# TensorE's per-quad work as a loop of three turns, with the values of the last two quads in other PSUM banks, in a sliding-window attention decode step

## The chip, the cores and the metric

The kernel runs on one core of a Trainium2 chip. The metric is the device time of one execution in microseconds (us).

## The reference

One token for each of 32 sequences attends to the last 512 positions of a cache of 2,048. There are 32 query heads over 8 key/value heads of width 128; all arrays are bfloat16.

```python
W = min(4096, max(256, Sk // 4))                      # 512
q = (x @ wq).reshape(B, Sq, Hq, Dh)...                # x 32x1x512, wq 512x4096
k = jnp.repeat(k_cache[:, :, Sk - W:, :], rep, axis=1)   # 32 x 8 x 512 x 128, rep 4
v = jnp.repeat(v_cache[:, :, Sk - W:, :], rep, axis=1)
p = softmax(einsum("bhqd,bhkd->bhqk", q, k) * Dh ** -0.5)
out = einsum("bhqk,bhkd->bhqd", p, v)... @ wo         # wo 4096x512
```

## The kernel before

The 32 sequences are worked on in eight quads of four. A quad's window of keys is one load of 4 MB (K), its window of values another (V). In both, the 128 partitions are sequence, key/value head and a quarter of the window: each partition holds 128 rows of 128 elements. `K_sb` and `V_sb` have two buffers each, for even and odd quads. `V_sb[1]` first holds the query weights (two loads of 2 MB at the very start), and `K_sb[0]` holds the output weights (4 MB as W0, W1 and W2) at the end.

For each quad q the steps have letters, which the orders use:

- T (VectorE, line 445): 32x32 transposes of K into `KT_sb`, in two halves `Tq.0` and `Tq.1`, both of which read the whole buffer.
- GpSimd (line 289) lays the queries of the quad out as a block diagonal `QBD`, two buffers.
- S (TensorE, line 331): scores in two halves, 16 matmuls each, into one PSUM bank `S_ps`.
- M, X, N: maximum (VectorE, 451, 453), exponential with row sums (ScalarE, 496), normalised probabilities as bfloat16 (VectorE, 457, 459).
- E (TensorE, 346): 16 matmuls that bring the probabilities to the rows of the values, into `EP_ps`; G (ScalarE, 503) copies them out.
- B (VectorE 465, ScalarE 509): eight instructions spread them into the block-diagonal `bd`, two buffers.
- P (TensorE, 361): probabilities times values, 128 matmuls in 32 groups of four; `P4.8.24` is groups 8 to 23 of quad 4. They accumulate in four banks `O_ps`.
- C (VectorE 470, ScalarE 514): four copies pick each head's own part out into `C_sb`, two buffers.
- F (TensorE, 373) and D (ScalarE, 518): four float32 matmuls fold the picks into one bank `F_ps`, and a copy puts them into `o_sel` as columns for the output projection.

After all quads TensorE multiplies `o_sel` by the output weights (line 393: 64 matmuls for W0, 48 for W1, 16 for W2), VectorE and ScalarE copy the result out, and SP stores it.

The order on each engine is written out by hand in the strings `PE_OPS`, `DVE_OPS` and `ACT_OPS`; TensorE's, VectorE's and ScalarE's programs are those strings unrolled. `needs()` gives the steps that an operation has to wait for, `ends` the value that a step's counting semaphore has when it is done, and `Waits` emits a wait only where an engine has not yet waited for as much. Loads are issued by SP alone, in the order of `LOADS`, and SP waits in that order too: a K of quad 2 or later waits for the second transpose half two quads before (line 228), a V for the last P two quads before (236), V1 for the query projection, and W0 for `T6.1` (242).

```python
LOADS = """
K0 K1 V0.0 K2 V1.0 K3 V2.0 K4 V3.0 K5 K6 V4.0 K7 V5.0 V5.1 V6.0 V6.1 V7.0 V7.1 W0 W1 W2
""".split()
V_PIECES = [1, 1, 1, 1, 1, 2, 2, 2]
```

So V0 to V4 come in one piece, V5 to V7 in halves. The eight PSUM banks are: scores 0, E 1, values 2 to 5, folds 6, output projection 7.

Of the kernel before, what the change touches and what calls it, by code (L numbers as in the profile page):

```python
# [17 lines left out]

PE_OPS = """
S0.0 S0.1 S1.0 S1.1 E0 E1 P0.0.32 S2.0 F0 S2.1 P1.0.12 E2 P1.12.32 F1 S3.0 S3.1 P2.0.12 E3  # L20
P2.12.32 F2 S4.0 S4.1 P3.0.12 E4 P3.12.32 S5.0 S5.1 S6.0 P4.0.4 E5 P4.4.8 S6.1 P4.8.24 E6 P4.24.32
F3 S7.0 P5.0.20 S7.1 P5.20.32 E7 F4 P6.0.32 F5 P7.0.32 F6 F7
"""
DVE_OPS = """
T0.0 T0.1 T1.0 M0 T1.1 N0 M1 N1 B0.0.4 B1.0.4 T2.0 T2.1 M2 N2 B2.0.4 T3.0 T3.1 M3 N3 B3.0.4 T4.0
T4.1 M4 N4 B4.0.4 T5.0 C3.2.3 T5.1 C3.3.4 T6.0 M5 T6.1 N5 B5.0.4 M6 N6 T7.0 C4.2.4 T7.1 B6.0.4 M7
N7 C5.2.4 B7.0.5 C6.2.4 C7.2.4
"""
ACT_OPS = """
X0 X1 G0 B0.4.8 G1 B1.4.8 C0.0.4 D0 X2 G2 B2.4.8 C1.0.4 D1 X3 G3 B3.4.8 C2.0.4 D2 X4 G4 B4.4.8  # L30
C3.0.2 X5 G5 B5.4.8 X6 G6 C4.0.2 B6.4.7 D3 B6.7.8 X7 C5.0.2 G7 B7.5.6 D4 B7.6.8 C6.0.2 D5 C7.0.2
D6 D7
"""
# [14 lines left out]
def bass_standalone__sliding_block_cached__sampling_kernel(  # L48
# [8 lines left out]
    B, Sq, D = x.shape  # L57
# [14 lines left out]

    orders = {"PE": ops_of(PE_OPS), "DVE": ops_of(DVE_OPS), "ACT": ops_of(ACT_OPS)}

    ends, total = {}, {}
    for eng, ops in orders.items():
        for op in ops:
            kind = op[0]
            total[eng, kind] = total.get((eng, kind), 0) + 1
            if kind in "BC":  # L80
                for i in range(op[2], op[3]):
                    ends[kind, op[1], i] = (eng, kind, total[eng, kind])
            elif kind == "P":
                for g in range(op[2], op[3]):
                    ends["P", op[1], g] = (eng, kind, total[eng, kind])
            else:
                ends[op] = (eng, kind, total[eng, kind])

    def needs(op):
        kind, q = op[0], op[1]  # L90
        spread = lambda q: [("B", q, h) for h in range(HKV)]
        picks = lambda q: [("C", q, r) for r in range(4)]
        d = []
        if kind == "T":
            d = [("S", q - 1, op[2])]
        elif kind == "S":
            d = [("T", q, op[2]), ("X", q - 1)]
        elif kind == "M":
            d = [("S", q, 1)]
        elif kind == "X":  # L100
            d = [("M", q), ("N", q - 1)]
        elif kind == "N":
            d = [("X", q), ("E", q - 1)]
        elif kind == "E":
            d = [("N", q), ("G", q - 1)]
        elif kind == "G":
            d = [("E", q)] + spread(q - NG)
        elif kind == "B":
            d = [("G", q), ("P", q - 2, 31)]
        elif kind == "P":  # L110
            d = spread(q) + picks(q - 1)
        elif kind == "C":
            d = [("P", q, 31), ("F", q - 2)]
        elif kind == "F":
            d = picks(q) + [("D", q - 1)]
        elif kind == "D":
            d = [("F", q)]
        return [ends[n] for n in d if n[1] >= 0]

    with ExitStack() as es:  # L120
# [47 lines left out]
        sem_v = [[sem(f"sem_v{i}_{j}") for j in range(max(V_PIECES))] for i in range(2)]  # L168
        sem_wo = [sem(f"sem_wo{i}") for i in range(len(WOP))]
        sem_out = sem("sem_out")  # L170
        names = (
            "pe_xT pe_q pe_Y dve_xT dve_q dve_QT dve_m dve_r dve_y dve_c act_q act_y act_warm "
            "pool_x pool_e pool_ei pool_q pool_f pool_m pool_j pool_qbd pool_fz"
        ).split()
        s = {n: sem(n) for n in names}
        op_sem = {key: sem("op_%s_%s" % key) for key in total}

        def v_waits(q, g0, g1):

            n = V_PIECES[q]  # L180
            for i in range(n):
                if g0 <= i * 32 // n < g1:
                    c = sum(1 for p in range(q % 2, q + 1, 2) if V_PIECES[p] > i)
                    yield i * 32 // n, sem_v[q % 2][i], 16 * c

# [33 lines left out]
        def _(sp):  # L219
# [3 lines left out]
            for op in ops_of(" ".join(LOADS)):  # L223
# [5 lines left out]
                elif kind == "V":  # L229
                    if q == 1:  # L230
                        sp.wait_ge(s["pe_q"], 8)
                    if q >= 2:
                        wait([ends["P", q - 2, 31]])
                    n = R // V_PIECES[q]
                    r0 = op[2] * n
                    sp.dma_start(  # L236
                        V_sb[q % 2][:, r0 * DH:(r0 + n) * DH], rows(v_cache, q, r0, r0 + n)
                    ).then_inc(sem_v[q % 2][op[2]], 16)
                else:
                    wait([ends["T", NQ - 2, 1]])  # L240
                    i0, i1 = WOP[q]
                    sp.dma_start(  # L242
                        wo_sb[:, i0:i1, :].rearrange("p i n -> p (i n)"),
                        wo_r[:, i0:i1, :].rearrange("p i n -> p (i n)"),
                    ).then_inc(sem_wo[q], 16)
# [8 lines left out]
        def _(pool):  # L254
# [27 lines left out]
            for q in range(NQ):  # L282
                if q >= 2:
                    wait([ends["S", q - 2, 1]])
                for b in range(4):
                    pr = slice(32 * b, 32 * b + 32)
                    if q or b:
                        pool.wait_ge(s["pool_qbd"], 4 * q + b)
                    pool.tensor_copy(  # L289
                        QBD[pr, q % 2].rearrange("p (w t) (h c) -> p w t h c", w=2, h=HKV)[  # L290
                            :, :, :, :, 4 * b:4 * b + 4],
                        QT_sb[pr, q].rearrange("p w (h e) t -> p w t h e", h=HKV),
                    ).then_inc(s["pool_qbd"], 1)

        @block.tensor
        def _(pe):
# [23 lines left out]
            def scores(q, w):  # L320
                if w == 0:
                    pe.wait_ge(s["pool_qbd"], 4 * q + 4)
                if q == 0 and w == 0:
                    pe.wait_ge(s["dve_q"], 4)
                    pe.wait_ge(s["act_q"], 4)
                for t in range(2):
# [232 lines left out]
```

## Time and profile before

| | |
|---|---|
| Timed runs (3) | 186.43 us median, 186.42 to 186.54 |
| Profiled execution: span from first to last instruction | 184.68 us (184.7 on the page) |
| Profiled execution's own total | not listed apart; the median of the timed runs is 1.75 us over the span |
| Busy: TensorE, its weight loads | 119.1 us (65%), 56.8 us (31%) |
| Busy: VectorE, ScalarE, GpSimd | 106.6 us (58%), 49.8 us (27%), 16.9 us (9%) |
| Mean granted TensorE clock | 0.823 |
| Moved by DMA | 75.80 MB in 3,584 packets, mean 410 GB/s |
| Costliest groups | transposes T 70.6 us (16 of 4.43 us), P 63.1 us (1,024 matmuls), S 25.3 us (256) |

Busy time is the time in which an engine has an instruction at work. The chain is the work that ended last, followed back from step to step to what released it. Queue q1 holds the kernel's loads and its store, q10 the loads of x, and the two queues of kind "instruction" bring program code to the engines. PE is TensorE, PEld its weight loads, DVE VectorE, ACT ScalarE, POOL GpSimd, SP SyncE.

### The profile page before, as it was taken

The numbers are of one execution on the slowest core, as the hardware profiler recorded it, in microseconds if no ns is written. First come the engines' busy times: TensorE is split into PE (matmuls) and PEld (weight loads), VectorE is DVE, ScalarE is ACT, GpSimd is POOL, SyncE is SP. The second block draws the span as 40 slices with busy tenths as digits, with TensorE's granted clock in tenths as the row PEclk, the third lists the DMA queues.
The fourth block names the chain that finished last, engine by engine and source line by source line (L and its number), as shares of the span: only waits on it lengthen the run. The fifth ranks groups of instructions, "written<-read, shape, count | busy, mean of one in ns | idle before, by whom it ended". The sixth has DMA issues, their size and how long they took to land.

```text
span 184.7 us, 3662 instructions
## 1 busy us (share of the span) xinstructions
PE 119.1 (65%) x1636; PEld 56.8 (31%) x1636; DVE 106.6 (58%) x106; ACT 49.8 (27%) x93; POOL 16.9 (9%) x52
## 2 busy tenths in 40 slices
PE   0089104447696795549944992441799899888872
PEld 0034000014452351304431350000345445444362
DVE  0031999994549631973299327999646996302031
ACT  3001300011935157001650162001062704502031
POOL 7900040202000200002000200020000000000000
PEclk9999955555599999657987699555579999999999
DMA  6999999999999999999999999999999999999970
GB/s 217 415 490 390 426 454 454 433 390 426 451 447 429 405 422 447 440 436 397 421 451 447 433 397 426 447 440 426 419 429 405 426 426 422 440 412 429 423 299 30
DMA packets 3584, 75.80 MB, mean 410 GB/s; under 512 B 432, under 2 KB 496, under 8 KB 624
## 3 DMA queue, kind: packets, MB, share of 16 engines
q1 hardware_dynamic: 3504, 75.53, 95.9%
q8 instruction: 13, 0.21, 0.5%
q10 hardware_dynamic: 64, 0.03, 0.1%
q14 instruction: 3, 0.02, 0.0%
HBM read 75.53 MB, written 0.03 MB: 409 GB/s over the span
## 4 chain that ended last, share of the span: by engine, by line
DMA 77%; DVE 13%; issue 3%; PE 3%; SPq 3%; DVEq 0%
DMA K_sb<-in_k_cache_dram 49%; DMA V_sb<-in_v_cache_dram 15%; DMA K_sb<-in_wo_dram 13%; DVE KT_sb L445 12%; PE ps L361 2%; SPq L236 1%; SPq L228 1%; SPq L242 1%; PE ps L331 1%; SPq L193 0%; DVE C_sb L470 0%; DVE maxv L451 0%; PE ps L393 0%; DVEq L120 0%; DVE P_bf L479 0%
## 5 line engine op out<-in xcount | busy, mean ns | idle before, releaser
L445 DVE STREAM_TRANSPOSE KT_sb<-K_sb 128x4096 f32<-128x4096 f32 x16 | 70.6, 4433 | 12.5 <-DMA K_sb<-in_k_cache_dram 12.4
L361 PE MATMUL ps<-V_sb,bd 32*128 32x512 bf16 x1024 | 63.1, 397 | 4.7 <-DMA V_sb<-in_v_cache_dram 2.9
L331 PE MATMUL ps<-KT_sb,QBD 128*32 128x512 bf16 x256 | 25.3, 532 | 39.7 <-DVE KT_sb L445 30.0
L361 PEld LDWEIGHTS ps<-V_sb,bd 32*128 32x128 bf16 x1024 | 27.0, 97 | 38.1 <-issue 12.3
L331 PEld LDWEIGHTS ps<-KT_sb,QBD 128*32 128x32 bf16 x256 | 6.6, 114 | 56.1 <-DVE KT_sb L445 37.0
L496 ACT ACTIVATE P_f<-ps,negmax 128x512 f32<-128x512 f32 x8 | 5.5, 687 | 63.1 <-DVE negmax L453 63.1
L509 ACT ACTIVATE bd<-PTc,mask 128x512 bf16<-128x512 bf16 x31 | 20.1, 710 | 0.3
L514 ACT ACTIVATE C_sb<-ps 32x512 f32<-32x512 f32 x22 | 12.9, 587 | 25.6 <-PE ps L361 25.4
L289 POOL COPY QBD<-QT_sb 32x128 bf16<-32x128 bf16 x32 | 9.2, 287 | 106.6 <-PE ps L331 90.2
L465 DVE TENSOR_SCALAR bd<-PTc,mask 128x512 bf16<-128x512 bf16 x33 | 9.3, 348 | 13.8 <-ACT PTc L503 13.8
L470 DVE COPY C_sb<-ps 32x512 f32<-32x512 f32 x10 | 6.9, 693 | 15.7 <-PE ps L361 15.6
L373 PE MATMUL ps<-C_sb,F_sb 128*128 128x128 f32 x64 | 10.0, 303 | 6.3 <-ACT C_sb L514 5.7
L346 PE MATMUL ps<-P_bf,E_sb 128*128 128x128 bf16 x128 | 11.0, 255 | 0.8 <-DVE P_bf L459 0.8
L373 PEld LDWEIGHTS ps<-C_sb,F_sb 128*128 128x128 f32 x64 | 8.3, 203 | 9.3 <-ACT C_sb L514 8.0
L346 PEld LDWEIGHTS ps<-P_bf,E_sb 128*128 128x128 bf16 x128 | 9.3, 116 | 4.9 <-DVE P_bf L459 2.8
L451 DVE TENSOR_REDUCE maxv<-ps 128x1 f32<-128x512 f32 x8 | 5.5, 686 | 7.3 <-PE ps L331 7.2
L503 ACT ACTIVATE PTc<-ps 128x512 bf16<-128x512 f32 x8 | 4.8, 594 | 18.2 <-PE ps L346 18.0
L313 PE MATMUL ps<-V_sb,bd 128*128 128x512 bf16 x32 | 8.5, 433 | 0.8 <-DVE bd L413 0.8
L301 PE MATMUL ps<-bd 32*128 32x128 bf16 x4 | 0.6, 296 | 9.2 <-DMA bd<-in_x_dram 9.2
L413 DVE CAST bd<-ps 128x512 bf16<-128x512 f32 x1 | 0.7, 692 | 9.8 <-PE ps L301 9.8
L434 DVE CAST KT_sb<-ps 128x512 bf16<-128x512 f32 x4 | 2.5, 684 | 6.0 <-PE ps L313 6.0
L490 ACT ACTIVATE KT_sb<-ps 128x512 bf16<-128x512 f32 x4 | 2.1, 603 | 14.0 <-PE ps L313 14.0
(29 smaller groups left out, 33.9 us busy)
## 6 DMA issues: line engine op xcount, KB each, us to landing
K_sb<-in_k_cache_dram SPq DMA_DIRECT2D x8, 4096.0 KB, 25.7
V_sb<-in_v_cache_dram SPq DMA_DIRECT2D x5, 4096.0 KB, 30.1
V_sb<-in_v_cache_dram SPq DMA_DIRECT2D x6, 2048.0 KB, 16.5
V_sb<-in_wq_dram SPq DMA_DIRECT2D x2, 2048.0 KB, 10.0
K_sb<-in_wo_dram SPq DMA_DIRECT2D x1, 2048.0 KB, 19.9
K_sb<-in_wo_dram SPq DMA_DIRECT2D x1, 1536.0 KB, 22.9
K_sb<-in_wo_dram SPq DMA_DIRECT2D x1, 512.0 KB, 23.6
out_dram<-P_bf SPq DMA_DIRECT2D x1, 32.0 KB, 1.5
```

The lines of the kernel that those rows point to most:

```text
L289: pool.tensor_copy(QBD[pr, q % 2].rearrange("p (w t) (h c) -> p w t h c", w=2, h=HKV)[:, :, :, :, 4 * b:4 * b + 4], QT_sb[pr, q].rearrange ...
L313: ins = pe.matmul(ps[:, n], lhsT=xT_sb[:, kt, :], rhs=wq_sb[:, kt, n * 512:(n + 1) * 512], start=kt == 0, stop=kt == DKT - 1, tile_positio ...
L331: ins = pe.matmul(S_ps[32 * c:32 * c + 32, :], lhsT=QBD[:, q % 2, 2 * w + t, c0:c0 + 32], rhs=KT_sb[:, w, :, KB * h:KB * h + KB, t], start ...
L346: ins = pe.matmul(EP_ps[:, e * R:(e + 1) * R], lhsT=E_sb[:, k, e].rearrange("p m j -> p (m j)"), rhs=P_bf[:, k * R:(k + 1) * R], start=k = ...
L361: ins = pe.matmul(O_ps[:, b, :], lhsT=bd[pr, q % 2, 4 * g:4 * g + 4].rearrange("p r h e -> p (r h e)"), rhs=V_sb[q % 2][pr, 512 * g:512 * ...
L373: ins = pe.matmul(F_ps[:, 0:P], lhsT=F_sb[:, d].rearrange("p h d -> p (h d)"), rhs=C_sb[:, q % 2, :, 32 * d:32 * d + 32], start=d == 0, st ...
L445: return dve.transpose(KT_sb[:, w].bitcast(F32).rearrange("p r c t -> p r (c t)"), K_sb[q % 2][:, :].bitcast(F32).rearrange("p (r w c) -> ...
L451: dve.tensor_reduce(maxv[:, q:q + 1], S_ps, AX.X, ALU.max).then_inc(s["dve_m"], 1)
L465: ins = dve.tensor_scalar(o, i, m, None, op0=ALU.mult)
L470: ins = dve.tensor_copy(*pick_args(q, r))
L509: ins = act.activation(o, i, ACTF.Copy, scale=m)
L514: ins = act.activation(*pick_args(q, r), ACTF.Copy)
```

## The change

TensorE's order becomes a head (`PE_HEAD`: the scores of quads 0 and 1, E0 and E1), six rounds of one form (`PE_ROUND`), and a tail (`PE_TAIL`). The six rounds are written as a loop on TensorE of three turns with two rounds in its body. In round q stand the fold of quad q-1, the scores of quad q+2 in two halves, E of quad q+2, and P of quad q in three parts between them. In round 0 the fold is a dry run (it folds a buffer that GpSimd has set to zero). Waits in the loop compare semaphores with registers that are worked out from the loop's counter; so that each wait is a linear function of the quad, semaphores are counted differently: the picks of both engines count on one semaphore, transposes on one for each half, D starts from 2, and the last of GpSimd's four copies of a quad counts on a semaphore of its own.

The values of quads 0 to 5 and 7 accumulate in banks 4 to 7, those of quad 6 in banks 0 to 3 (which hold scores, E, folds and the output projection otherwise). The fold of quad 5 goes to bank 4, the others to bank 2. All V loads come in two pieces, and in the order of loads K3, K4 and K5 each go ahead of the V that stood before them (V1, V2, V3). The orders of VectorE and ScalarE are written anew as well: on VectorE B of quad q stands behind the transposes of quad q+1, picks of quads 0 to 4 are all on ScalarE, and ScalarE's G0 stands ahead of X1.

```diff
-PE_OPS = """
-S0.0 S0.1 S1.0 S1.1 E0 E1 P0.0.32 S2.0 F0 S2.1 P1.0.12 E2 P1.12.32 F1 S3.0 S3.1 P2.0.12 E3
-P2.12.32 F2 S4.0 S4.1 P3.0.12 E4 P3.12.32 S5.0 S5.1 S6.0 P4.0.4 E5 P4.4.8 S6.1 P4.8.24 E6 P4.24.32
-F3 S7.0 P5.0.20 S7.1 P5.20.32 E7 F4 P6.0.32 F5 P7.0.32 F6 F7
-"""
+PE_HEAD = "S0.0 S0.1 S1.0 S1.1 E0 E1"
+PE_ROUND = "F{0} S{3}.0 P{1}.0.16 S{3}.1 P{1}.16.28 E{3} P{1}.28.32"
+PE_TAIL = "P6.0.16 F5 P6.16.32 P7.0.16 F6 P7.16.32 F7"
+ROUNDS = 6
 DVE_OPS = """
...
+T0.0 T0.1 T1.0 M0 T1.1 N0 M1 N1 B0.0.4 T2.0 T2.1 B1.0.4 M2 N2 T3.0 T3.1 B2.0.4 M3 N3 T4.0 T4.1
+B3.0.4 M4 N4 T5.0 T5.1 B4.0.4 M5 N5 T6.0 T6.1 B5.0.4 M6 N6 T7.0 T7.1 B6.0.4 M7 N7 C5.2.4 B7.0.4
+C6.2.4 C7.2.4
 """
 ACT_OPS = """
...
+X0 G0 X1 G1 B0.4.8 B1.4.8 X2 G2 C0.0.4 D0 B2.4.8 X3 G3 C1.0.4 D1 B3.4.8 X4 G4 C2.0.4 D2 B4.4.8 X5
+G5 C3.0.4 D3 B5.4.8 X6 G6 C4.0.4 D4 B6.4.8 X7 G7 C5.0.2 B7.4.8 D5 C6.0.2 D6 C7.0.2 D7
 """
...
-K0 K1 V0.0 K2 V1.0 K3 V2.0 K4 V3.0 K5 K6 V4.0 K7 V5.0 V5.1 V6.0 V6.1 V7.0 V7.1 W0 W1 W2
+K0 K1 V0.0 V0.1 K2 K3 V1.0 V1.1 K4 V2.0 V2.1 K5 V3.0 V3.1 K6 V4.0 V4.1 K7 V5.0 V5.1 V6.0 V6.1
+V7.0 V7.1 W0 W1 W2
...
-V_PIECES = [1, 1, 1, 1, 1, 2, 2, 2]
+V_PIECES = 2
...
-            d = spread(q) + picks(q - 1)
+            d = spread(q)
+            if q < NQ - 2:
+                d += picks(q - 1)
+            elif q == NQ - 2:
+                d += [("X", q + 1), ("G", q + 1), ("D", q - 2)]
+            else:
+                d += picks(q - 2) + [("D", q - 2)]
...
-        S_ps, EP_ps, O_ps, F_ps, Y_ps = ps[:, 0], ps[:, 1], ps[:, 2:6], ps[:, 6], ps[:, 7]
+        S_ps, EP_ps, F_ps, Y_ps = ps[:, 0], ps[:, 1], ps[:, 2], ps[:, 3]
+        def o_banks(q):
+            return ps[:, 0:4] if q == NQ - 2 else ps[:, 4:8]
+        def f_bank(q):
+            return ps[:, 4] if q == NQ - 3 else F_ps
...
+            for op in ops_of(PE_HEAD):
+                if op == ("E", 0):
+                    pe.wait_ge(s["pool_e"], 5)
+                do(op, plain)
+            with nc.Fori(0, ROUNDS, 2, engines=[mybir.EngineType.PE]) as i:
+                held = {}
+
+                def looped(q, a, b):
+                    if (a, a * q + b) not in held:
+                        held[a, a * q + b] = pe.snap(i * a + (a * q + b))
+                    return held[a, a * q + b]
+
+                for p in range(2):
+                    for op in ops_of(PE_ROUND.format(p - 1, p, p + 1, p + 2)):
+                        do(op, looped)
+            for op in ops_of(PE_TAIL):
+                do(op, plain)
```

More of the change, by code (lines that the diff above doesn't have):

```diff
@@ L10 @@
 AX = mybir.AxisListType
-PE_OPS = """
-S0.0 S0.1 S1.0 S1.1 E0 E1 P0.0.32 S2.0 F0 S2.1 P1.0.12 E2 P1.12.32 F1 S3.0 S3.1 P2.0.12 E3
-P2.12.32 F2 S4.0 S4.1 P3.0.12 E4 P3.12.32 S5.0 S5.1 S6.0 P4.0.4 E5 P4.4.8 S6.1 P4.8.24 E6 P4.24.32
-F3 S7.0 P5.0.20 S7.1 P5.20.32 E7 F4 P6.0.32 F5 P7.0.32 F6 F7
-"""
+PE_HEAD = "S0.0 S0.1 S1.0 S1.1 E0 E1"
+PE_ROUND = "F{0} S{3}.0 P{1}.0.16 S{3}.1 P{1}.16.28 E{3} P{1}.28.32"
+PE_TAIL = "P6.0.16 F5 P6.16.32 P7.0.16 F6 P7.16.32 F7"
+ROUNDS = 6
 DVE_OPS = """
-T0.0 T0.1 T1.0 M0 T1.1 N0 M1 N1 B0.0.4 B1.0.4 T2.0 T2.1 M2 N2 B2.0.4 T3.0 T3.1 M3 N3 B3.0.4 T4.0
-T4.1 M4 N4 B4.0.4 T5.0 C3.2.3 T5.1 C3.3.4 T6.0 M5 T6.1 N5 B5.0.4 M6 N6 T7.0 C4.2.4 T7.1 B6.0.4 M7
-N7 C5.2.4 B7.0.5 C6.2.4 C7.2.4
+T0.0 T0.1 T1.0 M0 T1.1 N0 M1 N1 B0.0.4 T2.0 T2.1 B1.0.4 M2 N2 T3.0 T3.1 B2.0.4 M3 N3 T4.0 T4.1
+B3.0.4 M4 N4 T5.0 T5.1 B4.0.4 M5 N5 T6.0 T6.1 B5.0.4 M6 N6 T7.0 T7.1 B6.0.4 M7 N7 C5.2.4 B7.0.4
+C6.2.4 C7.2.4
 """
 ACT_OPS = """
-X0 X1 G0 B0.4.8 G1 B1.4.8 C0.0.4 D0 X2 G2 B2.4.8 C1.0.4 D1 X3 G3 B3.4.8 C2.0.4 D2 X4 G4 B4.4.8
-C3.0.2 X5 G5 B5.4.8 X6 G6 C4.0.2 B6.4.7 D3 B6.7.8 X7 C5.0.2 G7 B7.5.6 D4 B7.6.8 C6.0.2 D5 C7.0.2
-D6 D7
+X0 G0 X1 G1 B0.4.8 B1.4.8 X2 G2 C0.0.4 D0 B2.4.8 X3 G3 C1.0.4 D1 B3.4.8 X4 G4 C2.0.4 D2 B4.4.8 X5
+G5 C3.0.4 D3 B5.4.8 X6 G6 C4.0.4 D4 B6.4.8 X7 G7 C5.0.2 B7.4.8 D5 C6.0.2 D6 C7.0.2 D7
 """
 LOADS = """
-K0 K1 V0.0 K2 V1.0 K3 V2.0 K4 V3.0 K5 K6 V4.0 K7 V5.0 V5.1 V6.0 V6.1 V7.0 V7.1 W0 W1 W2
+K0 K1 V0.0 V0.1 K2 K3 V1.0 V1.1 K4 V2.0 V2.1 K5 V3.0 V3.1 K6 V4.0 V4.1 K7 V5.0 V5.1 V6.0 V6.1
+V7.0 V7.1 W0 W1 W2
 """.split()
 X_PARTS = [(0, 2), (2, 8), (8, 18), (18, 32)]
-V_PIECES = [1, 1, 1, 1, 1, 2, 2, 2]
+V_PIECES = 2
 WOP = [(0, 16), (16, 28), (28, 32)]
@@ L71, in bass_standalone__sliding_block_cached__sampling_kernel, with counter @@
     NG = 4
-    orders = {"PE": ops_of(PE_OPS), "DVE": ops_of(DVE_OPS), "ACT": ops_of(ACT_OPS)}
-    ends, total = {}, {}
+    rounds = [PE_ROUND.format(q - 1, q, q + 1, q + 2) for q in range(ROUNDS)]
+    orders = {
+        "PE": ops_of(" ".join([PE_HEAD] + rounds + [PE_TAIL])),
+        "DVE": ops_of(DVE_OPS), "ACT": ops_of(ACT_OPS),
+    }
+    def counter(eng, op):
+        if op[0] == "T":
+            return ("DVE", "T%d" % op[2]), 1
+        if op[0] == "C":
+            return ("both", "C"), op[3] - op[2]
+        return (eng, op[0]), 1
+    ends, total = {}, {("ACT", "D"): 2, ("both", "C"): 4}
     for eng, ops in orders.items():
@@ L78, in bass_standalone__sliding_block_cached__sampling_kernel @@
             kind = op[0]
-            total[eng, kind] = total.get((eng, kind), 0) + 1
-            if kind in "BC":
+            key, n = counter(eng, op)
+            total[key] = total.get(key, 0) + n
+            if kind in "BP":
                 for i in range(op[2], op[3]):
[L82 to L85, printed above, removed]
+                    ends[kind, op[1], i] = key + (total[key],)
+            elif kind == "C":
+                for i in range(op[2], op[3]):
+                    ends[kind, op[1], i] = key + (4 * op[1] + 8,)
             else:
-                ends[op] = (eng, kind, total[eng, kind])
+                ends[op] = key + (total[key],)
     def needs(op):
@@ L115, in needs @@
             d = picks(q) + [("D", q - 1)]
+            if q == NQ - 1:
+                d += picks(q - 1)
         elif kind == "D":
             d = [("F", q)]
-        return [ends[n] for n in d if n[1] >= 0]
+        return [ends[n] for n in d if n in ends]
     with ExitStack() as es:
@@ L167, in bass_standalone__sliding_block_cached__sampling_kernel @@
         sem_k = [sem(f"sem_k{i}") for i in range(2)]
-        sem_v = [[sem(f"sem_v{i}_{j}") for j in range(max(V_PIECES))] for i in range(2)]
+        sem_v = [[sem(f"sem_v{i}_{j}") for j in range(V_PIECES)] for i in range(2)]
         sem_wo = [sem(f"sem_wo{i}") for i in range(len(WOP))]
@@ L171, in bass_standalone__sliding_block_cached__sampling_kernel @@
         names = (
-            "pe_xT pe_q pe_Y dve_xT dve_q dve_QT dve_m dve_r dve_y dve_c act_q act_y act_warm "
-            "pool_x pool_e pool_ei pool_q pool_f pool_m pool_j pool_qbd pool_fz"
+            "pe_xT pe_q pe_Y dve_xT dve_q dve_QT dve_m dve_r dve_y dve_c act_q act_y "
+            "pool_x pool_e pool_ei pool_q pool_f pool_m pool_j pool_qbd pool_quad pool_fz"
         ).split()
@@ L176, in bass_standalone__sliding_block_cached__sampling_kernel @@
         op_sem = {key: sem("op_%s_%s" % key) for key in total}
[L178 to L184, printed above, removed]
         for b0, b1 in X_PARTS:
@@ L233, in _ @@
                         wait([ends["P", q - 2, 31]])
-                    n = R // V_PIECES[q]
+                    n = R // V_PIECES
                     r0 = op[2] * n
@@ L270, in _ @@
             pool.memset(F_sb[:, :, :, :], 0.0).then_inc(s["pool_fz"], 1)
+            pool.memset(C_sb[:, 1], 0.0).then_inc(op_sem["both", "C"], 4)
             diag(E_id[:, :, :].rearrange("p e (b h) -> p e b h", b=4),
@@ L286, in _ @@
                     pr = slice(32 * b, 32 * b + 32)
-                    if q or b:
-                        pool.wait_ge(s["pool_qbd"], 4 * q + b)
+                    if b:
+                        pool.wait_ge(s["pool_qbd"], 3 * q + b)
+                    elif q:
+                        pool.wait_ge(s["pool_quad"], q)
                     pool.tensor_copy(
@@ L292, in _ @@
                         QT_sb[pr, q].rearrange("p w (h e) t -> p w t h e", h=HKV),
-                    ).then_inc(s["pool_qbd"], 1)
+                    ).then_inc(s["pool_quad" if b == 3 else "pool_qbd"], 1)
         @block.tensor
@@ L320, in scores @@
             def scores(q, w):
[L321 to L325, printed above, removed]
                 for t in range(2):
@@ L341, in to_value_rows @@
             def to_value_rows(q):
-                if q == 0:
-                    pe.wait_ge(s["pool_e"], 5)
                 for e in range(REP):
@@ L354, in pv @@
             def pv(q, g0, g1):
-                pieces = {g: (sm, n) for g, sm, n in v_waits(q, g0, g1)}
                 for g in range(g0, g1):
-                    if g in pieces:
-                        pe.wait_ge(*pieces[g])
                     for b in range(4):
@@ L361, in pv @@
                         ins = pe.matmul(
-                            O_ps[:, b, :],
+                            o_banks(q)[:, b, :],
                             lhsT=bd[pr, q % 2, 4 * g:4 * g + 4].rearrange("p r h e -> p (r h e)"),
@@ L369, in fold @@
             def fold(q):
-                if q == 0:
-                    pe.wait_ge(s["dve_c"], 7)
                 for d in range(4):
                     ins = pe.matmul(
-                        F_ps[:, 0:P],
+                        f_bank(q)[:, 0:P],
                         lhsT=F_sb[:, d].rearrange("p h d -> p (h d)"),
@@ L381, in _, with awaited @@
             run = {"S": scores, "E": to_value_rows, "P": pv, "F": fold}
-            for op in orders["PE"]:
-                wait(needs(op))
-                run[op[0]](*op[1:]).then_inc(op_sem["PE", op[0]], 1)
+            def awaited(op):
+                kind = op[0]
+                if kind == "S":
+                    yield op_sem["DVE", "T%d" % op[2]], 1, 1
+                    if op[2] == 0:
+                        yield op_sem["ACT", "X"], 1, 0
+                        yield s["pool_quad"], 1, 1
+                elif kind == "E":
+                    yield op_sem["DVE", "N"], 1, 1
+                    yield op_sem["ACT", "G"], 1, 0
+                elif kind == "P":
+                    if op[2] == 0:
+                        yield op_sem["DVE", "B"], 1, 1
+                        yield op_sem["ACT", "B"], 1, 1
+                        if op[1] >= NQ - 2:
+                            for end in needs(op):
+                                yield op_sem[end[:2]], 0, end[2]
+                    for i in range(V_PIECES):
+                        if op[2] <= i * 32 // V_PIECES < op[3]:
+                            yield sem_v[op[1] % 2][i], 8, 16 - 8 * (op[1] % 2)
+                elif kind == "F":
+                    yield op_sem["both", "C"], 4, 8
+                    yield op_sem["ACT", "D"], 1, 2
@@ new lines, in do @@
+            def do(op, value):
+                parts = [op]
+                if op[0] == "P":
+                    cuts = [op[2]] + [c for c in range(32 // V_PIECES, 32, 32 // V_PIECES)
+                                      if op[2] < c < op[3]] + [op[3]]
+                    parts = [op[:2] + c for c in zip(cuts, cuts[1:])]
+                for part in parts:
+                    for sm, a, b in awaited(part):
+                        if (v := value(op[1], a, b)) is not None:
+                            pe.wait_ge(sm, v)
+                    ins = run[op[0]](*part[1:])
+                ins.then_inc(op_sem["PE", op[0]], 1)
@@ new lines, in plain @@
+            def plain(q, a, b):
+                return a * q + b if a * q + b > 0 else None
+            pe.wait_ge(s["dve_q"], 4)
+            pe.wait_ge(s["act_q"], 4)
+            pe.wait_ge(s["dve_c"], 7)
+            for op in ops_of(PE_HEAD):
[11 more added lines that the diff above has]
+                        do(op, looped)
@@ L406, in pick_args @@
             pr = slice(32 * r, 32 * r + 32)
-            return C_sb[pr, q % 2], O_ps[pr, :, r * DH:(r + 1) * DH]
+            return C_sb[pr, q % 2], o_banks(q)[pr, :, r * DH:(r + 1) * DH]
         @block.vector
@@ L475, in _ @@
                 wait(needs(op))
-                run[op[0]](*op[1:]).then_inc(op_sem["DVE", op[0]], 1)
+                key, n = counter("DVE", op)
+                run[op[0]](*op[1:]).then_inc(op_sem[key], n)
             for c in (0, 2):
@@ L486, in _ @@
             act.wait_ge(s["pool_j"], 1)
-            act.activation(junk[:, 1:2], junk[:, 0:1], ACTF.Exp).then_inc(s["act_warm"], 1)
+            act.activation(junk[:, 1:2], junk[:, 0:1], ACTF.Exp).then_inc(op_sem["ACT", "D"], 2)
             for n in range(4):
@@ L519, in folded @@
                     o_sel[:, :, 4 * q:4 * q + 4],
-                    F_ps[:, 0:P].rearrange("p (b i) -> p i b", b=4), ACTF.Copy)
+                    f_bank(q)[:, 0:P].rearrange("p (b i) -> p i b", b=4), ACTF.Copy)
             run = {"X": exponential, "G": gather, "B": spread, "C": pick, "D": folded}
@@ L524, in _ @@
                 wait(needs(op))
-                run[op[0]](*op[1:]).then_inc(op_sem["ACT", op[0]], 1)
+                key, n = counter("ACT", op)
+                run[op[0]](*op[1:]).then_inc(op_sem[key], n)
             for c in (1, 3):
```

## The prediction

> **What bounds the kernel now.** I read the page first: busy slices, queues, chain.
>
> ```profile
> DMA  6999999999999999999999999999999999999970
> ...
> q1 hardware_dynamic: 3504, 75.53, 95.9%
> q8 instruction: 13, 0.21, 0.5%
> ...
> DMA 77%; DVE 13%; issue 3%; PE 3%; SPq 3%; DVEq 0%
> ```
>
> The DMA engines are busy in every slice from the second to the one before the last two; their queue takes 95.9% of sixteen engines' span, and 77% of the chain is DMA. TensorE (65%), VectorE (58%) and ScalarE (27%) matter only if they hold a load back. Next the end of the chain in order of time, and a table of the last stretches (last three columns: granted clock, DMA share, GB/s).
>
> ```profile
> 157.99 23.64 DMA K_sb<-in_wo_dram
> 181.64 0.04 issue
> 181.68 0.42 PE ps L393 x15
> 182.10 0.02 issue
> 182.12 0.28 DVE P_bf L479
> ```
>
> ```profile
> 172.00:175.00 3.00, 3.00 (x60) 1.43 (x56) 0.00 (x0) 0.00 (x0) 0.00 (x0) 1.00 0.97 412
> 175.00:178.00 3.00, 2.41 (x27) 1.82 (x20) 1.39 (x2) 1.45 (x3) 0.00 (x0) 1.00 0.95 393
> 178.00:180.00 2.00, 1.40 (x67) 1.03 (x66) 0.00 (x0) 0.28 (x1) 0.00 (x0) 1.00 0.48 193
> 180.00:181.00 1.00, 0.55 (x40) 0.55 (x44) 0.00 (x0) 0.00 (x0) 0.00 (x0) 1.00 0.23 94
> 181.00:182.00 1.00, 0.63 (x40) 0.39 (x28) 0.00 (x0) 0.00 (x0) 0.00 (x0) 1.00 0.09 20
> ```
>
> The last load sets the end, and it dies away over 3 us instead of stopping: the engines do not finish together. The trace's landing events (sixteen for each load, one for each DMA engine) say by how much. K0 lands from 22.48 to 23.06 us, a spread of 0.6. V4 lands from 129.34 to 131.23, 1.9. W2 lands from 178.34 to 181.64, 3.3: four engines at 181.26 to 181.64, four at 179.76 to 180.21, eight before 179.4. The earliest engine never pauses: K0 to K7 are twelve steps of 4 MB in 116.64 us, 9.72 each.
>
> What delays the others is in the packet records: 13 packets of 16,384 B on q8, 1.02 to 1.22 us each, one for about every 252 TensorE instructions issued (3,281 by the last). These are TensorE's instruction refills, twelve of them before W2 lands. After the first (46.59 us) one engine's landing of K2 is 1.3 us behind the next latest; the second and third each add an engine; after the ninth (151.40 us) one engine falls a further 1.4 us back, and after the twelfth there are four such. So the refills go round eight engines, each hit costs its engine about 1.3 us, and the end waits for an engine hit twice.
>
> **The change, part by part.** The sum is made against the profiled execution, span 184.68 us, on which the median of the timed runs (186.43) lies 1.75 us; no separate total of the profiled execution is listed. I add differences to 186.43.
>
> *Loop: fewer refills.* TensorE still issues as many matmuls, but its program shrinks: 132 matmuls ahead of the loop, 360 in a body of two rounds, 396 behind. Counting weight load and matmul apart, float32 folds twice as the trace does (64 records for 32) and some 45 waits and register steps, that is about 1,860 instructions, 7.3 pieces of 256, for 3,320 now. The trace has no loop, so the number of refills has to be bounded. Lower bound: each piece is fetched once, 7 refills, eight engines hit at most once. Upper bound: a jump back fetches its pieces anew. I place the four crossings of the first turn, five each for the second and third (target, its successor, three crossings) and three behind the loop: 17, so that one engine is hit three times. I take 7, since the body of 752 instructions spans three to four pieces and the rotation over eight engines looks like eight places of 16 KB, in which those pieces would still stand. The last landing then has the spread that V4 has after six refills and three smaller ones of 8 KB: 1.9 instead of 3.3, **-1.4 us**. The bounds are -1.4 and +1.3.
>
> [...]
>
> *Values in two pieces.* V0 to V4 become two loads of 2 MB each. A 32 KB packet takes 1.216 us in the median, two of 16 KB 1.224; with 8 packets an engine that is 0.06 us a load. By landings, V5 to V7 (halved already) take 29.35 us for 12 MB, 9.78 for 4 MB against 9.72, the same 0.06. Five loads: **+0.3 us**. Five more issues on SP of 0.6 us each run while loads are queued; they'd cost their 3.0 us only with an empty queue.
>
> *Order of loads.* K3 now stands ahead of V1 in SP's queue, so V1 goes out behind K3's wait for T1.1 (42.46 us before), with K3, instead of at 33.16. K0, K1 and V0 fill the engines till 41.9 and K2, issued at 32.6, till 51.6, so nothing runs dry: 0.
>
> *Rounds: when V buffers come free.* P0 to P5 now end behind E of the quad two ahead, so behind its transposes. The place to look is V7, which waits for P5:
>
> ```profile
> 121.50 0.54 SPq L228 DMA_DIRECT2D K_sb<-in_k_cache_dram  x1
> 122.07 34.77 SPq L236 DMA_DIRECT2D V_sb<-in_v_cache_dram  x6
> 156.89 1.54 SPq L242 DMA_DIRECT2D K_sb<-in_wo_dram  x3
> ```
>
> V7 goes out at 155.66 now, when P5 ends. Afterwards: K7 has landed at 141.3 (140.94 and the split's share); T7.0 and T7.1 take 8.8 to 150.2; P5.0.16 (3.6) runs beside T7.1; S7.1 1.05, to 151.3, beside which P5.16.28 follows with 2.8; maxes, exponential and norm take 2.6 from S7.1 (152.97 to 155.38 now with its handovers), to 154.1; E7 1.07; the last 16 matmuls 1.0: 156.2, with handovers 156.6. Issue to first packet is 1.0 us (first load: 0.73 to 1.76), so V7 is ready at 157.6. The first engine ends V6.1 at 159.0 (158.68 + 0.3). It holds by 1.4 us there, and by 3 us for the late engine that sets the end: 0. If that cover goes, each further us costs 1 us. Earlier buffers have more room: V6 is freed at about 137 with loads queued to 149.
>
> *Jumps, register waits.* A jump that misses would stall TensorE for a refill, 1.1 us and its wait for data packets of 1.2 us, so a few us; it stands ahead of F1 and of F3, behind which S4 and S6 wait for transposes that have some 4 us to go. A register step of TensorE has no row; the nearest are VectorE's sequencer step in the chain, 0.02 us, and an issue on SP, 0.6. There are some ten steps and waits a round; by the lower end (the step is no transfer) they cost nothing, by the upper one 6 us a round, which would be the fourth rival. 0 in the sum.
>
> *P6 and P7 in other banks; folds in the rounds; F7's bank.* Now P6 waits for C5 (0.6 us) and P7 for C6 (0.6), F7 waits for D6 until 177.20. Afterwards P7's first half is not behind C6, and F7 not behind D6. But W0's matmuls (178.69) and their 2.36 us of work (1.08 + 0.85 + 0.43) end at 181.05 without the load, 0.6 ahead of its landing: the tail waits for W2 in both. P7.16.32 would start at V7.1's landing, 170.8, end at 174.4; picks 1.5, fold 1.2, D7 0.3: W0 at 177.6, done with 112 matmuls by 180.2 with W1 landed, before W2 at 180.6. So the gain of 1.4 isn't lost there, and the end after landing (0.42, 0.28, output 1.5 and its handovers, 3.04 in all) stays. 0.
>
> *ScalarE and VectorE orders.* G0 ahead of X1 delays N1 by about 0.9 us, long before K2 lands at 53.5; all C but the last go to ScalarE, 2.39 us a quad, with 73% idle. 0.
>
> Sum: 186.43 - 1.4 + 0.3 = 185.3.
>
> **Rivals.**
>
> 1. *As many refills as now* (9 to 16 before the end: pieces counted by what is issued, or only one fetched anew a turn). An engine is hit twice; only the split counts: 186.7. For it: refills follow issue closely in this trace, 252 apart. Against: nothing in it jumps back.
>
> 2. *Jumps back fetch anew, 17 to 24 refills: slower.* Place: the two jumps and the crossings behind them; price: 1.3 us for the third hit, so 186.43 + 0.3 + 1.3 = 188.0. It decides from the seventeenth refill before about 181 us. For it: all 13 crossings fetched something, none was spared. Against: eight engines in rotation, if they mean eight places.
>
> 3. *A jump empties eight prefetched places,* eight refills for each of two jumps over those of the crossings, some 30: four hits, two more than now, 186.43 + 0.3 + 2.6 = 189.3. For it: TensorE has no refill in the 9 us ahead of the span, when four others of 8 KB run, so much may be fetched ahead.
>
> 4. *V7 late:* TensorE at half clock (S takes 1.90 for 1.05, 48 matmuls of P up to 4.45 for 2.8) and stalls push P5's end to 161: the gain goes and 1 to 2 us more, about 187.5. Against: P5.0.16 keeps TensorE busy beside T7.1.
>
> **How the numbers follow.** Chances: forecast 0.52; rival 1 0.15; rival 2 0.17; rival 3 0.07; rival 4 0.09. The likeliest alone ranges from 184.9 to 185.8 (spread 1.6 to 2.2, split 0.2 to 0.5). The whole range goes from 184.9 to 188.2, which takes in rival 2 and leaves out rival 3 and the edges. This kernel's measurement tells 0.2% (0.37 us) from no change: faster is the forecast and a little, 0.53; the same is most of rival 1, 0.11; slower the rest, 0.36.
>
> **What would show it.** In the profile afterwards: q8 with 7 or 8 packets for 13 (17 or more: rival 2; 30: rival 3); W2's sixteen landings within about 2 us instead of 3.3, and the DMA row falling off more steeply at the end; more data packets at equal bytes; V7 issued at 156 to 157.5 with no dip in the DMA row; F7 following C7 at once. I am wrong if the refills are not fewer, if their engines aren't distinct, or if the earliest engine's steps break before W.

## The result: 187.31 us, 0.5% slower, and where the time went

| | median us | lowest to highest |
|---|---|---|
| before (5 runs) | 186.43 | 186.41 to 186.54 |
| after (5 runs) | 187.31 | 186.84 to 187.88 |

The ratio is 1.0048, interval 1.0035 to 1.0061. The profiled execution of the changed kernel is its slowest, 187.88 us with a span of 186.1. The forecast was 185.3, so 2.0 us have to be found. The page of the kernel after first:

```profile
DMA  6999999998999999999999999999999999899970
GB/s 212 415 493 409 394 451 412 433 479 380 433 451 451 391 426 426 444 419 416 463 409 416 426 465 430 398 426 437 465 405 416 426 426 437 282 426 416 431 324 17
...
q1 hardware_dynamic: 4224, 75.53, 95.9%
q8 instruction: 7, 0.11, 0.2%
```

Two things are to be seen. q8 has 7 packets for 13: the refills went as forecast. And there is a dip to 282 GB/s near 160 us, in the midst of a row that stays above 400 around it. The chain, in order of time, says who made it:

```profile
156.49 1.00 PE ps L361 x16
157.49 1.00 PE ps L373 x16
158.49 0.02 issue
158.51 0.54 SPq L255
...
161.68 21.38 DMA K_sb<-in_wo_dram
```

The last 16 matmuls of P5 (line 373) end at 158.49 us, and only then SP issues V7 (line 255), 2.9 us later than before (155.66). Its first packet starts at 159.83, 1.32 us after the issue; by then ten of the sixteen DMA engines had ended V6.1, the first at 159.11 (V6.1's landings). For them the queue ran dry. Here is that stretch by windows (last columns: granted clock, DMA share, GB/s):

```profile
158.00:159.00 1.00, 0.95 (x24) 0.32 (x16) 0.48 (x1) 0.61 (x2) 0.00 (x0) 1.00 0.66 279
159.00:160.00 1.00, 1.00 (x24) 0.53 (x20) 0.95 (x3) 0.96 (x3) 0.00 (x0) 1.00 1.25 328
160.00:161.00 1.00, 1.00 (x24) 0.59 (x20) 1.00 (x4) 1.00 (x3) 0.00 (x0) 1.00 0.24 66
```

A packet counts in the window in which it starts, so 1.25 and 0.24 belong together: 13 packets that start between 159.8 and 160.5 take 0.28 to 0.94 us longer than the usual 0.61. The kernel's first fifteen packets (from 1.76 us on) take 1.11 to 1.61 us. So starting up cost about what it costs at the beginning.

### The profile page after: what moved, and what is told of

It is laid out like the page before. It is cut to its first block, busy times and chain, and to the rows that moved or that the text cites. A ratio compares the mean times of both kernels' runs of the same rounds, so it can differ in the third digit from the quotient of the medians.

```text
span 186.1 us, 3720 instructions
## 1 busy us (share of the span) xinstructions
PE 122.4 (66%) x1644; PEld 59.0 (32%) x1644; DVE 102.7 (55%) x101; ACT 52.2 (28%) x98; POOL 17.5 (9%) x53
## 4 chain that ended last, share of the span: by engine, by line
DMA 56%; DVE 20%; PE 15%; issue 4%; SPq 2%; ACTq 1%; ACT 0%; DVEq 0%
DMA K_sb<-in_k_cache_dram 41%; DVE KT_sb L513 16%; DMA K_sb<-in_wo_dram 11%; PE ps L373 7%; PE ps L335 4%; DMA bd<-in_x_dram 4%; PE ps L348 3%; DVE QT_sb L505 2%; DVE KT_sb L502 1%; SPq L261 1%; SPq L255 1%; ACTq L206 1%; PE ps L361 1%; ACT P_f L565 0%; DVE maxv L519 0%
## 5 line engine op out<-in xcount | busy, mean ns | idle before, releaser
L373 PE MATMUL ps<-V_sb,bd 32*128 32x512 bf16 x1024 | 64.2, 398 | 1.8 <-DMA V_sb<-in_v_cache_dram 1.7
L373 PEld LDWEIGHTS ps<-V_sb,bd 32*128 32x128 bf16 x1024 | 26.1, 98 | 38.3 <-issue 16.6
L383 PE MATMUL ps<-C_sb,F_sb 128*128 128x128 f32 x72 | 14.0, 354 | 14.1 <-ACT C_sb L583 12.6
L583 ACT ACTIVATE C_sb<-ps 32x512 f32<-32x512 f32 x26 | 15.3, 588 | 9.3 <-PE ps L373 9.1
L383 PEld LDWEIGHTS ps<-C_sb,F_sb 128*128 128x128 f32 x72 | 12.0, 252 | 17.9 <-ACT C_sb L583 9.0
L538 DVE COPY C_sb<-ps 32x512 f32<-32x512 f32 x6 | 4.2, 693 | 16.8 <-PE ps L373 16.8
L361 PE MATMUL ps<-P_bf,E_sb 128*128 128x128 bf16 x128 | 10.2, 243 | 2.1 <-DVE P_bf L527 2.1
L361 PEld LDWEIGHTS ps<-P_bf,E_sb 128*128 128x128 bf16 x128 | 8.6, 110 | 5.7 <-DVE P_bf L527 4.9
L587 ACT ACTIVATE o_sel<-ps 128x128 bf16<-128x128 f32 x8 | 2.2, 278 | 16.8 <-PE ps L383 16.8
```

The costliest lines, as they stand in the source:

```text
L361: ins = pe.matmul(EP_ps[:, e * R:(e + 1) * R], lhsT=E_sb[:, k, e].rearrange("p m j -> p (m j)"), rhs=P_bf[:, k * R:(k + 1) * R], start=k = ...
L373: ins = pe.matmul(o_banks(q)[:, b, :], lhsT=bd[pr, q % 2, 4 * g:4 * g + 4].rearrange("p r h e -> p (r h e)"), rhs=V_sb[q % 2][pr, 512 * g: ...
L383: ins = pe.matmul(f_bank(q)[:, 0:P], lhsT=F_sb[:, d].rearrange("p h d -> p (h d)"), rhs=C_sb[:, q % 2, :, 32 * d:32 * d + 32], start=d == ...
L583: ins = act.activation(*pick_args(q, r), ACTF.Copy)
```

## TensorE in the last round, before and after

TensorE's instructions in order of time, first the kernel before, then after (start, length, line, what, how many):

```profile
145.46 1.05 PE L331 MATMUL ps<-KT_sb,QBD 128*32 128x512 bf16 x16 [0.29 <-DVE KT_sb L445]
147.09 3.63 PE L361 MATMUL ps<-V_sb,bd 32*128 32x512 bf16 x64 [0.58 <-DVE C_sb L470]
150.89 1.04 PE L361 MATMUL ps<-V_sb,bd 32*128 32x512 bf16 x16 [0.17 <-DMA V_sb<-in_v_cache_dram]
151.87 1.05 PE L331 MATMUL ps<-KT_sb,QBD 128*32 128x512 bf16 x16
152.85 2.77 PE L361 MATMUL ps<-V_sb,bd 32*128 32x512 bf16 x48
155.55 1.07 PE L346 MATMUL ps<-P_bf,E_sb 128*128 128x128 bf16 x16
```

```profile
145.86 1.90 PE L348 MATMUL ps<-KT_sb,QBD 128*32 128x512 bf16 x16 [2.72 <-DVE KT_sb L513]
147.69 5.12 PE L373 MATMUL ps<-V_sb,bd 32*128 32x512 bf16 x64
152.74 1.05 PE L348 MATMUL ps<-KT_sb,QBD 128*32 128x512 bf16 x16
153.72 2.77 PE L373 MATMUL ps<-V_sb,bd 32*128 32x512 bf16 x48
156.42 1.07 PE L361 MATMUL ps<-P_bf,E_sb 128*128 128x128 bf16 x16
157.42 4.72 PE L373 MATMUL ps<-V_sb,bd 32*128 32x512 bf16 x80
```

Before, the same 16 score matmuls of S7.0 take 1.05 us and the first 64 of P5 3.63; after, 1.90 and 5.12. Ahead of S7.0 TensorE now idles for 2.72 us (0.29 before), and ahead of F4, in the same round, for 2.49. S7.1 stands behind P5.0.16 in TensorE's order and starts at 152.74, although its keys were transposed at 150.1. In addition E7 (1.07) comes ahead of P5's end now; before it came behind. There is no idle time left between 145.86 and 158.49: TensorE itself sets when V7 may be loaded.

## Experiments

Theory A, formed from the two traces: the refills saved what was forecast, but V7 is issued too late, the DMA queue empties, and that costs more. Theory B: the loop, its register waits or the split loads cost by themselves, and the late V7 is harmless, since the late engines set the end. Each run is compared with runs of the kernel before on the same chip (medians 186.32 to 186.35).

**V7 early.** The values of quad 7 go to another buffer, which takes away the wait on P5:

```diff
+        def v_buf(q):
+            return K_sb[1] if q == NQ - 1 else V_sb[q % 2]
...
-                    if q >= 2:
+                    if q == NQ - 1:
+                        wait([ends["T", q, 1]])
+                    elif q >= 2:
                         wait([ends["P", q - 2, 31]])
```

(Lines 256 and 376 of the changed kernel then use `v_buf(q)`, and V7 has semaphores of its own.)

> The changed kernel, but the values of quad 7 go into the key buffer of odd quads, which is free once T7.1 is done, so SP issues V7 behind T7.1 (about 150.4 us) and no longer behind P5 (158.5). Theory A (the late V7 empties the DMA queue and is what costs; the seven refills do save): the DMA row has no dip, the sixteen landings of W2 lie within about 2 us of each other, W2's last landing is near 180.6, and the time is 185.2 to 185.5, that is 0.5 to 0.7% under the kernel before. Theory B (the loop, its register waits or the split loads cost by themselves, the late V7 is harmless because the late engines set the end): the time stays at 187.0 to 187.5.

Measured: 185.25 us (185.12 to 185.72), ratio 0.9940, interval 0.9928 to 0.9953. V7 goes out at 149.99. The same windows as above, of this kernel:

```profile
158.00:159.00 1.00, 0.98 (x24) 0.32 (x17) 0.45 (x1) 0.61 (x2) 0.00 (x0) 1.00 0.89 377
159.00:160.00 1.00, 1.00 (x24) 0.54 (x20) 0.95 (x3) 0.96 (x3) 0.00 (x0) 1.00 1.11 475
160.00:161.00 1.00, 1.00 (x24) 0.59 (x20) 1.00 (x4) 1.00 (x2) 0.00 (x0) 1.00 1.00 426
```

No packet is lengthened there. W2 lands from 178.56 to 180.33, a spread of 1.8. TensorE is as late as before this edit (P5 ends at 158.5 in both traces), so what lies between the two is the cost of the late issue: 2.0 us by their ratios to the kernel before (1.0048 and 0.9940). Theory B falls.

**No loop,** with V7 late and with V7 early:

```diff
-            with nc.Fori(0, ROUNDS, 2, engines=[mybir.EngineType.PE]) as i:
...
+            for q in range(ROUNDS):
+                for op in ops_of(PE_ROUND.format(q - 1, q, q + 1, q + 2)):
+                    do(op, plain)
```

> The changed kernel with the six rounds written out and no loop; all orders, loads and buffers stay. Theory A: q8 has 13 packets again, V7 is issued at about 158.5 as with the loop, the DMA queue empties all the same, and since the engines are brought level there, only the refills behind it count: the time is that of the changed kernel or a little more, 187.0 to 187.9. Theory B (the loop itself costs): 186.5 to 186.8, the split loads alone.

> Both edits: no loop, and V7 into the key buffer behind T7.1. Theory A: no dip, 13 refills, one engine hit twice, spread of W2's landings 3.3 us: 186.6 to 186.9, so that the loop is worth 1.4 us against the run with V7 early and the loop. Theory B: the same 186.5 to 186.8 as without the loop and V7 late, and less than the looped kernel with V7 early.

Measured, medians in us, with the two runs above:

| | loop (7 refills) | written out (13 refills) |
|---|---|---|
| V7 behind P5 | 187.31 | 187.25 (186.67 to 187.57) |
| V7 behind T7.1 | 185.25 | 186.70 (186.57 to 186.88) |

The loop is worth 1.45 us with V7 early and nothing with V7 late. The landings show why. With V7 early and the rounds written out, W2 lands from 178.62 to 182.04, with four engines at 181.70 and later, as in the kernel before. With V7 late and the loop (the traced execution, of 187.88 us), 14 of the 16 landings of V7.0 lie between 165.72 and 166.17, although V6.1's had ended from 159.11 to 160.91: the engines that were ahead lost their lead in the gap and the lengthened packets. What a saved refill had gained an engine was lost there, and the refills at 166.28 and 174.76 now each hit an engine that was as late as any: 13 landings of V7.1 lie up to 171.04, 12 of W0 up to 175.94, and the next follow at 172.29 and 177.16. Two more engines fell behind on further lengthened packets. The records name no engine, but a packet of 0.97 us at 161.18 ends where one of 1.29 starts (162.14), and one of 1.24 at 161.80 where one of 1.38 starts (163.03), so I read them as two pairs; V7.0's last two landings are 167.41 and 168.40. W2's last four landings are 182.07, 182.20, 182.23 and 183.05.

**E last.** One edit of the round's form, which takes E7 from in front of P5's end:

```diff
-PE_ROUND = "F{0} S{3}.0 P{1}.0.16 S{3}.1 P{1}.16.28 E{3} P{1}.28.32"
+PE_ROUND = "F{0} S{3}.0 P{1}.0.16 S{3}.1 P{1}.16.32 E{3}"
```

> The changed kernel with E moved behind P in each round (F, S.0, P.0.16, S.1, P.16.32, E). This takes E7's 1.0 us from in front of P5's end and nothing else. Theory A: V7 is issued 1.0 us earlier, at 157.5, its first packet comes at about 158.8, just ahead of 159.1, where the first engine ends V6.1; the queue is not or hardly empty and most of the 1.9 us comes back: 185.3 to 186.3. Theory B: no change, 187.0 to 187.5.

Measured: 185.50 us (185.20 to 185.91, the traced execution 185.26), ratio 0.9960, interval 0.9947 to 0.9973. V7 is issued at 156.67, earlier than expected: 1.0 us from E, and P5.0.16 took 4.60 us in this execution. So V7 may come about here without a dry queue, while 1.8 us later it costs 1.8 us. It isn't all or nothing, though. Here too six packets that start from 158.42 to 158.76 take 0.12 to 0.38 us longer than 0.61, before the first engine ends V6.1 (158.90), and W2 still lands from 178.65 to 180.34. Why packets lengthen before any engine has run dry stays open.

**TensorE kept busy.** Whether the length of S7.0 and P5.0.16 is the granted clock's doing or the order's was tested with added matmuls that nobody reads:

```diff
-PE_ROUND = "F{0} S{3}.0 P{1}.0.16 S{3}.1 P{1}.16.28 E{3} P{1}.28.32"
+PE_ROUND = "H10 F{0} H14 S{3}.0 P{1}.0.16 S{3}.1 P{1}.16.28 E{3} P{1}.28.32"
```

(`Hn`: n matmuls of 128x128 by 128x512 into the bank of the output projection, which is free then.)

> The changed kernel with 24 more matmuls of 512 columns in each round, 10 ahead of the fold and 14 behind it, whose results nobody reads; they fill the stretches in which TensorE waits for the picks and for the next transpose. Theory A (P5 ends late because S7.0 and the first half of P5 run at half clock, and S7.1 stands behind them): in the last round S7.0 takes 1.05 us for 1.90 and the 64 matmuls of P5 3.6 for 5.1, P5 ends near 156.2, V7 is issued near 156.3 and the time is 185.2 to 185.8. Theory B (it is the order alone, not the clock): P5 ends no earlier than 158 and the time stays at 187.0 to 187.6, or more for the added work.

Measured: 185.28 us (185.09 to 186.18, three of the ten above 186; the traced execution 185.09), ratio 0.9954, interval 0.9937 to 0.9970, with more work on TensorE. Its timeline in the last round:

```profile
140.06 3.19 PE L393 MATMUL ps<-E_sb 128*128 128x512 bf16 x14
145.63 1.05 PE L348 MATMUL ps<-KT_sb,QBD 128*32 128x512 bf16 x16 [2.38 <-DVE KT_sb L522]
146.62 3.63 PE L373 MATMUL ps<-V_sb,bd 32*128 32x512 bf16 x64
150.18 1.05 PE L348 MATMUL ps<-KT_sb,QBD 128*32 128x512 bf16 x16
```

The order is that of the changed kernel, and S7.0 and P5.0.16 take 1.05 and 3.63 again, although TensorE was idle for 2.38 us just before. The profile also shows the clock itself. The same two microseconds, first of the changed kernel, then of this run (last columns: granted clock, DMA share, GB/s):

```profile
146.00:148.00 2.00, 2.00 (x20) 0.45 (x16) 2.00 (x1) 0.00 (x0) 0.00 (x0) 0.50 0.96 410
```

```profile
146.00:148.00 2.00, 2.00 (x44) 0.81 (x36) 2.00 (x1) 0.00 (x0) 0.00 (x0) 1.00 1.02 434
```

In the changed kernel the granted clock is 0.50 from 142 to 150 us. It falls between 140 and 142 (0.63 there), while TensorE waits for the picks ahead of F4 and before its wait for T7.0. In this run, as in the kernel before, it is 1.00 from 138 to 158. So it was the clock, and the added matmuls kept it up; its mean over the span is 0.931 here for 0.823. S7.1 starts at 150.18 and V7 is issued at 155.95.

**The split's price.** The kernel before with V0 to V4 in halves:

```diff
-V_PIECES = [1, 1, 1, 1, 1, 2, 2, 2]
+V_PIECES = [2] * 8
```

> The kernel before, with V0 to V4 loaded in two halves as V5 to V7 are, and nothing else. The forecast's term for the split is +0.3 us: 186.6 to 186.9 against 186.4. If the split costs nothing, the same as before within 0.1 us.

Measured: 187.15 us (186.66 to 187.51), ratio 1.0038, interval 1.0026 to 1.0050: more than either expectation. The trace shows two things that are not the split's own price. P5's first 80 matmuls take 5.93 us (the granted clock is 0.50 from 148 to 150) and V7 is issued at 157.03, and five packets about 158.5 to 159.4 are lengthened by 0.27 to 0.61. W2's last landing is 181.73, only 0.09 later than before; and then TensorE pauses within W1's matmuls:

```profile
182.16 0.53 PE L393 MATMUL ps<-K_sb,o_sel 128*32 128x128 bf16 x24 [0.87 <-issue]
```

"issue" means that nothing the profile records held it. The last refill before it starts at 179.65 and takes 1.06 us; that TensorE waited for code is a guess that no run tests. So this run does not give the term. Two others do: written out with V7 early against the kernel before, both with 13 refills and no dry queue, is 186.70 against 186.32, +0.38 (the other parts of the change are in it as well); and the next one.

**V7 early and V0 to V5 whole:**

> The changed kernel with V7 in the key buffer of odd quads (issued behind T7.1), and V0 to V5 loaded whole again, V6 and V7 in halves. Theory A with the split's term: 0.3 to 0.35 us under the run with V7 early and all values in halves (185.25), so 184.8 to 185.0, 0.7% or more under the kernel before. If the split costs nothing: 185.2 to 185.3.

```diff
-                    n = R // V_PIECES
+                    n = R // V_PIECES if q >= NQ - 2 else R
```

(`LOADS` has V0 to V5 once each, and the rounds wait for one semaphore a load.) Measured: 188.49 us (188.08 to 188.98), ratio 1.0113, interval 1.0093 to 1.0133. As a kernel this is 3.5 us more than expected; as a measure of the split it serves: W2 lands from 178.07 to 180.01 where the halves had 178.56 to 180.33, so 0.3 to 0.5 us for six loads. But TensorE is too late to use it:

```profile
131.24 5.32 PE L379 MATMUL ps<-V_sb,bd 32*128 32x512 bf16 x64 [2.40 <-DMA V_sb<-in_v_cache_dram]
...
181.94 1.98 PE L472 MATMUL ps<-K_sb,o_sel 128*32 128x128 bf16 x128 [0.37 <-ACT o_sel L598]
```

P.0.16 stands ahead of S.1 in each round and waits for the whole V, 2.40 us in round 4, so the rounds slip, P5 ends at 162.4, and the output projection starts at 181.94, when all weights have landed (the last at 180.01). The halves aren't optional with this form of round.

**Both cures,** V7 early and E last:

> V7 into the key buffer of odd quads and E behind P in each round. Theory A (once V7 is out in time the end is the latest DMA engine's, and TensorE's order no longer matters): the time of the run with V7 early alone, 185.1 to 185.4. Rival (both edits still add up, since TensorE's tail sets the end): under 185.0.

Measured: 185.22 us (185.12 to 185.36), ratio 0.9938, interval 0.9924 to 0.9952; the same as with V7 early alone. This and the kernel with V7 early beat both kernels, the one before by 0.6%.

**How much code is kept.** The forecast of 7 refills rested on an estimate of eight places of 16 KB, made from refills of 16,384 B that seemed to go round eight engines. Two runs with a longer loop body, made longer by small matmuls at the head of each round (196 and 388 of them, 128x128, unread). The bodies have about 1,536 and 2,304 instructions; at one refill for about 252, as in the kernel before, these are some six and nine pieces:

> A look at q8 alone. The changed kernel with 196 small matmuls (128x128, not read by anyone) at the head of each round, so that the loop's body grows from 752 to about 1,536 instructions, 6.0 pieces of 16 KB, and TensorE's program to 10.3 pieces. The time is longer for the added work and says nothing. If eight pieces are kept: 10 or 11 refills, none of them in the second and third turn. If fewer are kept (four or so): the body's pieces are fetched again in each turn, 20 or more.

> The same with 388 small matmuls a round: the body has about 2,304 instructions, 9.0 pieces. If eight pieces are kept: the body no longer fits, the second and third turn fetch it anew, about 30 refills. If more than eight are kept: 13 or 14.

The instruction queue of each:

```profile
q8 instruction: 10, 0.16, 0.3%
```

```profile
q8 instruction: 35, 0.57, 0.8%
```

With six pieces in the body the refills come at 50.2 to 95.1 us, seven of them in the first turn, then none until 191.4 us, behind the loop. With nine pieces they come in every turn. There the jumps back show on TensorE as well, before the first matmul of the second and of the third turn:

```profile
119.91 5.02 PE L393 MATMUL ps<-E_sb 128*128 128x128 bf16 x87 [2.76 <-issue]
189.50 23.45 PE L393 MATMUL ps<-E_sb 128*128 128x128 bf16 x388 [2.57 <-issue]
```

The turns before end at 117.15 and 186.93, and a refill starts at 117.18 and at 187.03. With six pieces no idle time stands in these places (96.05 and 140.43). So the body of six pieces was not fetched again behind a jump (ten refills), and the one of nine was (35). That fits the estimate of eight places; by these two counts alone six or seven would do as well, and no run shows the number itself.

## Why the prediction was wrong, point by point

- *What bounds the kernel:* right. In most traces where V7 came in time, TensorE's last matmuls start 0.04 us after W2's last landing, as before. The exceptions are runs in which TensorE was late for it: V0 to V5 whole, the kernel before in halves with its pause, and the traced execution of V7 early (185.72, the longest of its five). There the output projection took 3.32 us at a granted clock of 0.50 from 179 to 181 and ended at 181.26, 0.93 after W2's landing; in the traces of before and after it ends 0.46 and 0.47 after it.
- *Refills, -1.4:* right in count (7; the estimated 1,860 instructions, at one refill for about 252 as in the trace before, are 7.4), in the spread of W2's landings (1.8 for 3.4 written out) and in size (-1.45 between the two runs with V7 early). Rivals 1 to 3 fall with the count of 7. That refills go round eight engines fits the landings (four late engines with twelve refills, none with seven and V7 early), but no record names the engine.
- *Split, +0.3:* right within what could be measured, 0.3 to 0.5.
- *When V buffers come free, 0: this step failed.* It put S7.1 at 150.2, with "P5.0.16 (3.6) runs beside T7.1" and S7.0 not counted at all. They took 1.90 and 5.05 us one after the other, so S7.1 ended at 153.79 instead of 151.3. From there to P5's end the forecast had 4.9 us and it took 4.7. P5 ended at 158.49 for 156.2 to 156.6, and the cover of 1.4 us was gone. The term that was wrong is the clock: with it kept up, S7.1 starts at 150.18 and V7 goes out at 155.95, within some 0.3 us of the forecast, so leaving out S7.0 did little harm. The durations taken were those of the kernel before in the same place, where the granted clock was 1.00; the slow values, 1.90 and up to 4.45 for 48 matmuls, stood in the same trace and were named in the fourth rival.
- *The price of a late V7:* failed too. The forecast gave the late engines, which set the end, 3 us of cover from 157.6 on, so to about 160.6, and nothing would have been lost with V7's first packet at 159.83. It cost 2.0. The traces say how: V7.0's engines are level at 166.17, where V7 early's last landing of V7.0 is 165.64, so 0.5 is lost by then; behind that a refill makes one more engine late (14 landings of V7.0 lie up to 166.17 and two later, 13 of V7.1 up to 171.04 and three from 172.29 on), by about 1.25 us, close to the 1.3 of the kernel before. With 1.32 us to the first packet and the first engine free at 159.11, the queue runs dry from an issue at about 157.8 on; this is an estimate, with no run between 157.03 (kernel before in halves) and about 158.1 (rounds written out).
- *The fourth rival* was what happened, at 0.09 and about 187.5. Its mechanism was right, but P5's end at 158.5 was enough for it, not only at 161. The argument against it, that P5.0.16 keeps TensorE busy beside T7.1, failed: the granted clock was 0.50 from 142 us on, before S7.0 began (145.86).
- *Jumps and register waits, other banks, tail:* no cost seen. F7 (178.44) follows the picks at once, as said. With nine pieces the two jumps back did cost what was said, a few us (2.76 and 2.57 of idle time, a refill at each); here no refill starts between 87.39, in TensorE's wait for the picks ahead of the second turn, and 166.28, behind the loop.
- *Range:* it held the measured time (184.9 to 188.2); the forecast's sign was wrong.

## What to carry to other kernels

Where the DMA queue is the bound, look for the load with the least lead, and time the chain that releases its buffer with the slow durations of each engine, not the good ones: here an order that left TensorE idle ahead of a stretch ran that stretch at half the granted clock (0.50 from 142 to 150 us, where it was 1.00 in the kernel before). A queue that runs dry can lose more than the gap: here V7's first packet came 0.7 us after the first engine was free, and it cost 2.0, since the engines that were ahead lost their lead and with it what the saved refills had gained. Give the last loads a buffer that comes free early; here the other operand's buffer did, at no cost in memory.

## What the runs showed of the hardware that was not expected

With a loop body of about 1,536 instructions no refill came in the second and third turn (10 in all); with one of about 2,304 refills came in every turn (35), and before the second and the third turn TensorE stood idle for 2.76 and 2.57 us. While the granted clock was 0.50, 16 score matmuls took 1.90 us for 1.05 and 64 of P 5.12 for 3.63; with 24 added matmuls a round it was 1.00 in the last round, and they took 1.05 and 3.63. And 13 packets of the late V7 took 0.28 to 0.94 us longer than the usual 0.61, like the kernel's first fifteen (0.49 to 1.00 longer).
